# Products with w_in1 in float32 on 64x32 tiles of the array, blocks of 384 tokens, and a second batch that starts like the first

## The chip, the cores and the metric

The kernel runs on one core of a Trainium2 chip. The core has five engines with queues of their own: TensorE (PE; its weight loads are a row of their own, PEld), VectorE (DVE), ScalarE (ACT), GpSimd (POOL) and SyncE (SP), which issues all DMAs here. The metric is the device time of one execution in microseconds (us).

## The reference, cut to what matters

```python
def sm_attn(qq, kk, vv):              # softmax over the keys
    s = scale * np.matmul(qq, kk.transpose(0, 1, 3, 2))
    ...
p_packed = sm_attn(p, k, v)           # 32 packed queries p over 576 keys
out = sm_attn(q, p_packed, p_packed)  # 576 queries q over 32 packed rows
x = out, as (8*576, 512)
h = x @ w_in1;  x = (h * sigmoid(h)) @ w_out1     # 512 -> 2048 -> 512
h = x @ w_in2;  y = (h * cos(h)) @ w_out2         # 512 -> 2048 -> 512
```

There are 8 batches, 8 heads of 64, 576 rows. All four weight matrices arrive as float64, so the kernel reads them as pairs of 32-bit words and makes float32 of them ("conversion").

## The kernel before, in words

**Numbers in two parts.** Large products are made from a high part rounded to float32r and a low part that is what is left: `mm3` (lines 485 to 489) issues low x high, high x low, high x high. `split` (501) makes the parts with a copy on ACT or DVE and a subtraction on DVE or POOL.

**Attention.** Per batch b and half g of the heads, `stage1` (703) makes the 64 packed rows per pair of heads (`ppf`), and `stage2` (769) the probabilities of the 576 queries over them (`a2`). The attention's output is never formed: since x = a2 @ packed, the first MLP's h is a2 @ (packed @ w_in1). So `products` (815) multiplies the packed rows with w_in1, for a quarter s of w_in1's columns at a time (512), and puts the result as two parts into slots of W (`mslot`). For this `stationary` (759) places the packed rows of both batches of a pair in the zero-padded tile L; `parts` (805) moves the two batches' halves out of the bank, 64 partitions at a time: a copy and a subtraction each. Batch 0 alone takes `sole_products` (826).

**Batch 0 and the others.** Batch 0 uses the class `Boot` (629): q and k come on 96 partitions, six rows of 64 on each (1.5 KB runs), and TensorE turns them by products with the identity. All others use `Steady` (585): they come in runs of 32 numbers to the tiles kin, and VectorE turns them (STREAM_TRANSPOSE big<-kin).

**Conversion.** `decode` (517) reads 128x512 float64 numbers into wd (or wde at the start), and makes float32 in wy with one ACT, three or four DVE and one POOL instruction, then `split`s it. Units: 16 of w_in1 (both parts spilled to w1dram, 512 KB, and loaded again for each pair by `w1_load`, 800), 16 of w_out1 (to W), 32 of w_in2 and w_out2 (`w2_unit`, to w2dram).

**First MLP.** A step is one block of tokens and one of 16 column chunks fc: six matmuls into hb (`first`, 853), tanh on ACT, a multiplication on DVE (gf), `split` into g, and three steps later twelve matmuls into the four banks acc. A block is half a batch, 288 tokens, so a pair of batches takes 4 x 16 = 64 steps, and 4 pairs 256. In pair 0 the steps go by quarters of fc, and each quarter's sums are kept apart (ydram, ypart). At a block's end two banks are moved out by ACT and two by DVE into one tile ysb, and one DMA takes it to DRAM.

**Second MLP.** 9 blocks of 512 tokens times 16 steps of 24 matmuls of 512 columns.

**What sets the order.** The program is recorded by `Plan` (79) and put in one static order by a list scheduler with prices (`price`, 151), due times (`due_first`, 964, from DUE, 410), release times, and copies that may go to either of two engines (`either`). Every engine's queue then runs in this order; a waiting instruction holds up all behind it on its engine, SP's DMA issues too. The loop at 1052 to 1074 records, for each pair, the steps of the first MLP, the attention of the next pair's batches (`seconds`), its products (from step 48 of 64 on), and in the last pair the w2 units.

Of the kernel before, what the change touches and what calls it, by code (L numbers as in the profile page):

```python
# [74 lines left out]
class Op:  # L75
    __slots__ = ("choice", "engine", "emit", "cost", "issue", "due", "release", "after", "before")


class Plan:
# [9 lines left out]
    ISSUE, WIRE = 500, 650  # L89

# [60 lines left out]
    def price(self, engine, f, out, ins):  # L151
# [32 lines left out]
    def add(self, engine, f, emit, args, kw):  # L184
# [11 lines left out]
        self.record(engine, run, [self.region(x) for x in outs], [self.region(x) for x in ins], cost, issue)  # L196

# [7 lines left out]
    def record(self, engine, emit, outs, ins, cost, issue):  # L205
# [5 lines left out]
        else:  # L211
# [4 lines left out]
            op.after, op.before, op.choice = [], [], {}  # L216
# [56 lines left out]
    def schedule(self, rank, reverse=False):  # L273
# [40 lines left out]
        while done < n:  # L314
# [5 lines left out]
            for e in queue:  # L320
# [7 lines left out]
                end = free[e] = t + o.cost  # L328
# [50 lines left out]
def attention_mlps_kernel(  # L379
# [17 lines left out]
    P = 128  # L397
    HALF = S // 2
    NB = S // 32
# [10 lines left out]
    DUE = [38e3, 212e3, 392e3, 572e3, 738e3]  # L410
# [33 lines left out]

    ydram = dram.tile([KC, P, NT], F32, name="ydram")
    ypart = [dram.tile([KC, P, 2 * S], F32, name=f"ypart{i}") for i in range(1, NG)]
    w1dram = dram.tile([KC, KC, P, 2, 512], F32, name="w1dram")
# [33 lines left out]
    mask = const.tile([P, 2], F32, name="mask")  # L481
    half_pi = const.tile([P, 1], F32, name="half_pi")
    pbd = const.tile([P, H // 2, 2 * NP], F32, name="pbd")
# [27 lines left out]
    early_wy = tiles(stage, [P, WIDE], I32, "wye", 1)  # L511
# [5 lines left out]
    def decode(src, dst=None, spill=None):  # L517

        wd, y = rings["wd"](), rings["wy"]()
        flat = wd.rearrange("p f t -> p (f t)")  # L520
        parts = flat.rearrange("p (t f) -> p t f", t=2).bitcast(F32R)
        DMA.dma_start(flat.rearrange("p (c f) -> p c f", c=src.shape[1]) if len(src.shape) == 3 else flat, src)
        lo, hi = wd[:, :, 0], wd[:, :, 1]
        yf = y.bitcast(F32)
# [13 lines left out]
    def w1_unit(s, hp, dst):  # L538

        decode(w_in1[hp * P : (hp + 1) * P, 1024 * s : 1024 * (s + 1)], dst, w1dram[s, hp])  # L540

    def wout1_unit(c):
        decode(w_out1[c * P : (c + 1) * P], W[c])

    def w2_unit(c, i):
# [4 lines left out]
        decode(src, None, w2dram[c, i])  # L550
# [11 lines left out]
    Ls = ring(tiles(att, [P, 2, H // 2, 2, 2 * NP], F32R, "L", 1))  # L562
    a2s = ring(tiles(a2p, [P, 2, S], F32R, "a2", 4))

    def place_p(b):
# [8 lines left out]
        for h2 in range(2):  # L574
            r = slice(64 * h2, 64 * h2 + 64)
            V.transpose(pbd[r, :, NP * h2 : NP * h2 + NP], t[r].rearrange("p j d -> p (j d)"))
# [52 lines left out]
    class Boot:  # L629
# [11 lines left out]
        def load(self, n, src):  # L641
            for g in range(2):
                for j in range(2):
# [3 lines left out]
                        src[0, h].rearrange("h (r c) d -> r h (c d)", c=NCH),  # L647
# [37 lines left out]
    def half(b, j):  # L685

        return (b + j) % 2

    ppf = {}
    L = {}  # L690
    a2 = {}

    def scores(keys, queries, rows, bank):

        sts = [bank()[:, :HALF] for _ in range(2)]
        with plan.together():
            for hf, st in enumerate(sts):
                c = slice(hf * HALF, (hf + 1) * HALF)
                for j in range(2):
                    T.matmul(st[rows(j)], keys[:, j], queries[j][:, c], start=True, stop=True)  # L700
        return sts

    def stage1(b, g, bank, mem):
# [5 lines left out]
        sts = scores(pbd[:, 2 * g : 2 * g + 2], kt, lambda j: slice(64 * j, 64 * j + 64), bank)  # L709
# [22 lines left out]
        with plan.together():  # L732
            for c in range(n):
                for j in range(2):
                    for h2 in range(2):
                        h = 32 * (2 * j + h2)
# [12 lines left out]
            mask.unsqueeze(2).to_broadcast([P, 2, D]),  # L749
# [9 lines left out]
    def stationary(b, g):  # L759

        if (b // 2) not in L:
            L[b // 2] = Ls()
        t = ppf[b, g]
        for j in range(2):
            hi, lo = (L[b // 2][:, x, 2 * g + j, half(b, j)] for x in range(2))
            copy(hi, t[:, j])
            combine(lo, t[:, j], f32(hi), ALU.subtract)

    def stage2(b, g, bank, mem):
# [4 lines left out]
        rows = lambda j: slice(64 * half(b, j), 64 * half(b, j) + 64)  # L774
        for hf, st in enumerate(scores(ppf[b, g], qt, rows, bank)):
            V.transpose(sf[:, hf * HALF : (hf + 1) * HALF], st)
# [344 lines left out]
```

## Time and profile before

| | us |
|---|---|
| median of 3 runs | 1641.14 (1639.12 to 1641.47) |
| profiled execution | 1641.7 |
| its span, first to last instruction | 1639.9 |
| TensorE busy | 1578.5 (96%) |
| VectorE busy | 1187.8 (72%) |
| ScalarE busy | 803.8 (49%) |
| GpSimd busy | 343.3 (21%) |

Busy is the time in which an engine has an instruction at work. Matmuls are pipelined, so TensorE can be busy and slower than it could be: the distance between the starts of matmuls tells its pace. Groups of instructions are named output<-inputs by the program's tiles, without buffer numbers. A float32 matmul stands as two instructions in the trace where it runs on a tile of the array.

### The profile page before, as it was taken

The page shows a single profiled execution, that of the slowest core. Times are in us where ns is not written, and L with a number is a line of the kernel's source. Part 1 is how long each engine was busy: PE and PEld are TensorE (multiplying, and loading weights), DVE is VectorE, ACT ScalarE, POOL GpSimd, SP SyncE. Part 2 cuts the span into 40 slices and gives each one's busy share as a digit, 9 for nine tenths or more (in the row PEclk, how much of TensorE's full clock was granted, in tenths as well). Part 3 has the DMA queues.
Part 4 walks back from the last instruction along what each step waited for, and adds up shares of the span by engine and source line. Part 5 has one row for each costly group of instructions (what it writes and reads, how often), then busy time and mean ns, then how long its engine had stood idle before and what let it go on. Part 6 is the DMA issues. An engine that isn't in the chain of part 4 may idle for free.

```text
span 1639.9 us, 25508 instructions
## 1 busy us (share of the span) xinstructions
PE 1578.5 (96%) x9570; PEld 1374.1 (84%) x9570; DVE 1187.8 (72%) x2157; ACT 803.8 (49%) x1584; POOL 343.3 (21%) x311
## 2 busy tenths in 40 slices
PE   8777999999988999999999999999999999999999
PEld 7667988899888999999988888888878888888887
DVE  6999688888688766756356767666676867676665
ACT  5665565645455454644344444444444444444444
POOL 2556232233133411002001101010221111120000
PEclk9889999999999999999999999999999999999999
DMA  8666777854687445524350101000020302010000
GB/s 205 190 236 160 205 203 201 275 168 145 152 221 236 149 115 110 182 83 137 143 195 0 52 1 39 14 26 27 20 71 1 110 20 90 6 47 1 13 14 26
DMA packets 238140, 175.74 MB, mean 107 GB/s; under 512 B 176320, under 2 KB 202688, under 8 KB 238016
## 3 DMA queue, kind: packets, MB, share of 16 engines
q1 hardware_dynamic: 238016, 174.11, 36.1%
q8 instruction: 75, 1.23, 0.3%
q14 instruction: 49, 0.40, 0.1%
HBM read 122.95 MB, written 51.12 MB: 106 GB/s over the span
## 4 chain that ended last, share of the span: by engine, by line
PE 63%; DVE 9%; issue 3%; DMA 2%; ACT 2%; POOL 1%; SPq 0%; DVEq 0%; POOLq 0%; ACTq 0%
PE acc L191 34%; PE hb L191 16%; PE sb L191 7%; PE mb L191 6%; DVE r L191 2%; DVE g L191 1%; ACT r L191 1%; DVE wd L191 1%; DVE big L191 1%; DVE wy L191 1%; DMA kin<-in_q 1%; DVE w L191 1%; DVE gf L191 1%; DVE n L191 1%; DMA yst<-ydram 1%
## 5 line engine op out<-in xcount | busy, mean ns | idle before, releaser
L191 PE MATMUL acc<-g,w 128*128 128x288 f32 x3072 | 472.8, 299 | 12.9 <-DVE ysb L191 5.3
L191 PE MATMUL acc<-w,g 128*128 128x512 f32 x1728 | 473.2, 394 | 2.2 <-DVE o L191 1.4
L191 PEld LDWEIGHTS acc<-g,w 128*128 128x128 f32 x3072 | 432.8, 190 | 27.5 <-DVE ysb L191 6.9
L191 PEld LDWEIGHTS acc<-w,g 128*128 128x128 f32 x1728 | 323.5, 187 | 81.3 <-DVE o L191 3.4
L191 PE MATMUL hb<-a,w 128*128 128x288 f32 x1536 | 264.7, 304 | 29.6 <-DVE w L191 9.7
L191 PEld LDWEIGHTS hb<-a,w 128*128 128x128 f32 x1536 | 227.0, 193 | 45.1 <-DVE gf L191 12.2
L191 ACT ACTIVATE r<-r 128x512 f32<-128x512 f32 x144 | 91.1, 633 | 339.2 <-DVE r L191 339.1
L191 PE MATMUL hb<-y,w 128*128 128x512 f32 x864 | 241.0, 391 | 0.0
L191 POOL TENSOR_TENSOR g<-r,g 128x512 fp32r<-128x512 f32 x49 | 64.9, 1324 | 611.3 <-ACT g L191 611.3
L191 PEld LDWEIGHTS hb<-y,w 128*128 128x128 f32 x864 | 162.1, 188 | 35.2
L191 ACT CAST g<-gf 128x288 fp32r<-128x288 f32 x233 | 100.3, 433 | 157.3 <-PE acc L191 102.0
L191 DVE TENSOR_TENSOR g<-gf,g 128x288 fp32r<-128x288 f32 x173 | 94.6, 548 | 81.3 <-ACT g L191 78.3
L191 DVE SCALAR_TENSOR_TENSOR gf<-gf,hb 128x288 f32<-128x288 f32 x256 | 113.5, 447 | 39.2 <-ACT gf L191 37.7
L191 ACT ACTIVATE gf<-hb 128x288 f32<-128x288 f32 x256 | 104.2, 409 | 69.2 <-PE hb L191 64.7
L191 POOL TENSOR_TENSOR g<-gf,g 128x288 fp32r<-128x288 f32 x83 | 75.7, 912 | 294.9 <-ACT g L191 267.5
L191 DVE SCALAR_TENSOR_TENSOR r<-n,r 128x512 f32<-128x512 f32 x144 | 126.6, 879 | 2.8
L191 PE MATMUL sb<-y,w 128*128 128x512 f32 x432 | 122.5, 391 | 0.0
L191 PE MATMUL mb<-y,w 128*128 128x512 f32 x432 | 121.6, 391 | 0.0
L191 DVE TENSOR_TENSOR r<-r,hb 128x512 f32<-128x512 f32 x72 | 49.5, 687 | 83.3 <-ACT r L191 83.2
L191 ACT ACTIVATE r<-r,half_pi 128x512 f32<-128x512 f32 x144 | 104.3, 724 | 4.2
L191 PEld LDWEIGHTS sb<-y,w 128*128 128x128 f32 x432 | 81.0, 188 | 17.2
L191 PEld LDWEIGHTS mb<-y,w 128*128 128x128 f32 x432 | 81.0, 188 | 17.1
(176 smaller groups left out, 1809.9 us busy)
## 6 DMA issues: line engine op xcount, KB each, us to landing
w<-w1dram SPq DMA_DIRECT2D x52, 512.0 KB, 4.4
w2dram<-wd SPq DMA_DIRECT2D x32, 512.0 KB, 3.4
w<-w2dram SPq DMA_DIRECT2D x32, 512.0 KB, 5.4
wd<-in_moe_w_in SPq DMA_DIRECT2D x24, 512.0 KB, 4.9
wd<-in_moe_w_out SPq DMA_DIRECT2D x20, 512.0 KB, 4.4
ydram<-ysb SPq DMA_DIRECT2D x16, 576.0 KB, 3.5
yst<-ydram SPq DMA_DIRECT2D x36, 256.0 KB, 2.7
out<-o SPq DMA_DIRECT2D x36, 256.0 KB, 2.0
```

The lines of the kernel that those rows point to most:

```text
L191: run = lambda: emit(*[real(x) for x in args], **{k: real(x) for k, x in kw.items()})
```

## The change

Products with w_in1: the packed rows stay float32 (ppf), w_in1 stays float32 (no parts; 256 KB per spill and load), and each batch, head pair and head is a matmul of its own of 64 rows and 32 columns of the array. L, `stationary`, `parts`, `sole_products` are gone; a bank holds 128 partitions of one batch and is moved out whole. `place(b, h2)` swaps the two heads' places for odd batches, in masks, pbd and stage1. Blocks are 384 tokens: three per pair, of which the middle one spans both batches (twelve hb matmuls of 192 columns), so 48 steps a pair, 192 in all; each block's four evictions go to ACT or DVE as the planner likes, into two tiles of a quarter each, with a DMA each. Batch 1 uses Boot and its tiles. The w2 units are released at the planner's 380 us. Its prices and DUE change, and it counts DVE as slowed by a busy POOL.

```diff
@@ prices and schedule
-            passes = 1 if ins[0].dtype == F32R else 4
-            return passes * n / 2.4 * (out.shape[0] / 128) + (14 if out.shape[0] == 128 else 24), 0
+            if ins[0].dtype == F32R:
+                return n / 2.4 + 14, 0
+            return n * out.shape[0] / 128 * (1.67 if out.shape[0] == 128 else 1.2 if ins[0].shape[0] > 64 else 0.6) + 10, 0
...
+                if e == self.DVE and o.sbuf and not reverse and free[self.POOL] > t:
+                    both = min(free[self.POOL] - t, o.cost / self.SHARED)
+                    end += both * (1 - self.SHARED)
...
-    DUE = [38e3, 212e3, 392e3, 572e3, 738e3]
+    DUE = [40e3, 205e3, 378e3, 550e3, 718e3]
@@ conversion
-        d = parts if dst is None else dst
-        split(d, yf)
-        if spill is not None:
-            DMA.dma_start(spill, f32(d))
+        return flat
+
+    def decode_parts(src, dst=None):
+        y = rings["wy"]()
+        flat = decode(src, y)
+        d = flat.rearrange("p (t f) -> p t f", t=2).bitcast(F32R) if dst is None else dst
+        copy(d[:, 0], y.bitcast(F32))
+        V.tensor_tensor(d[:, 1], y.bitcast(F32), f32(d[:, 0]), ALU.subtract)
+        return d
...
+    def w1_unit(s, hp, w):
+        decode(w_in1[hp * P : (hp + 1) * P, 1024 * s : 1024 * (s + 1)], w)
+        DMA.dma_start(w1dram[s, hp], w)
@@ products
-        for hp in range(KC):
-            w = ws[hp] if ws else w1_load(s, hp)
-            bank = (mb, sb)[hp % 2]
-            mm3(bank, heads(L[pr], hp), (w[:, 0], w[:, 1]), True, True)
+    def products(s, bs, ws=None):
+        ws = ws or [w1_load(s, hp) for hp in range(KC)]
+        for kc in range(2):
+            banks = {b: (mb, sb)[(kc + i) % 2] for i, b in enumerate(bs)}
+            with plan.together():
+                for b in bs:
+                    for j in range(2):
+                        for h2 in range(2):
+                            r, c = slice(64 * h2, 64 * h2 + 64), 32 * place(b, h2)
+                            T.matmul(
+                                banks[b][64 * j + c : 64 * j + c + 32],
+                                ppf[b, kc][r, j, c : c + 32],
+                                ws[2 * kc + j][r],
+                                start=True,
+                                stop=True,
+                            )
             for b in bs:
-                r = 64 * half(b, hp % 2)
-                parts(b, hp // 2, s, slice(r, r + 64), bank)
+                m = mslot(b, kc, s)
+                copy(m[:, 0], banks[b])
+                V.tensor_tensor(m[:, 1], banks[b], f32(m[:, 0]), ALU.subtract)
@@ steps of the first MLP
-    ysbs = ring(tiles(gp, [P, KC, HALF], F32, "ysb", 1))
+    ysbs = ring(tiles(gp, [P, TA], F32, "ysb", 2))
...
+        for b in range(2):
+            t0, t1 = max(blk * TA, b * S), min((blk + 1) * TA, (b + 1) * S)
+            if t0 >= t1:
+                continue
+            for kc in range(2):
+                m = mslot(b, kc, fc // 4)
+                a = a2[2 * pr + b, kc]
+                c = slice(t0 - b * S, t1 - b * S)
+                mm3(h[:, t0 - blk * TA : t1 - blk * TA], (m[:, 0, o : o + P], m[:, 1, o : o + P]), (a[:, 0, c], a[:, 1, c]), kc == 0, kc == 1)
...
             for dm in range(KC):
-                if dm % 2:
-                    V.tensor_scalar(t[:, dm], acc[dm][:, :HALF], 0.5, None, op0=ALU.mult)
-                else:
-                    A.activation(t[:, dm], acc[dm][:, :HALF], AF.Copy, scale=0.5)
+                t = ysbs()
+                with plan.either():
+                    A.activation(t, acc[dm][:, :TA], AF.Copy, scale=0.5)
+                    V.tensor_scalar(t, acc[dm][:, :TA], 0.5, None, op0=ALU.mult)
+                DMA.dma_start(dst[dm, :, t0 : t0 + TA], t)
...
-    ysts, yst = lates("yst", F32, 2)
+    ysts, yst = lates("yst", F32, 1)
@@ recording
-    firsts(1, steady, [bank, bank])
-    stationaries(1)
-    products(0, 0, (1,), ws)
-    seconds(1)
+    boot.load("k", k, 1)
+    boot.load("v", v, 1)
+    boot.load("q", q, 1)
+    firsts(1, boot, [bank, bank])
+    products(0, (1,), ws)
+    for g in range(2):
+        stage2(1, g, bank, boot)
...
+            plan.release = LATER
             for c in range(FC):
                 for i in range(2):
                     w2_unit(c, i)
+            plan.release = 0.0
...
-            if o == (31 if pr else 55):
+            if o == (31 if pr else 43):
                 seconds(b0 + 2)
-            if o >= 48 and o % 4 == 3:
-                products(pr + 1, (o - 48) // 4, (b0 + 2, b0 + 3))
+            if o >= 32 and o % 4 == 3:
+                products((o - 32) // 4, (b0 + 2, b0 + 3))
```

On PE, at the products of pair 0 with a later quarter of w_in1 (mb and sb are the two banks, w10 and w11 tiles of w_in1, ppf0 and ppf2 the packed rows of batches 0 and 1), there stands before:

```order
L191 MATMUL acc3_90<-g1_147,w3_98 128x288
L191 MATMUL mb_93<-w10_140,L0_135 128x512 x2
L191 MATMUL sb_94<-w11_141,L0_135 128x512
L191 MATMUL mb_93<-w10_140,L0_135 128x512
L191 MATMUL sb_94<-w11_141,L0_135 128x512 x2
L191 MATMUL hb0_91<-a23_139,w28_102 128x288
```

and now:

```order
L194 MATMUL acc3_90<-g0_150,w3_98 128x384
L194 MATMUL mb_93<-w10_140,ppf0_132 32x512 x2
L194 MATMUL mb_93<-w11_141,ppf0_132 32x512 x2
L194 MATMUL sb_94<-w10_140,ppf2_134 32x512 x2
L194 MATMUL sb_94<-w11_141,ppf2_134 32x512 x2
L194 MATMUL hb0_91<-a22_138,w24_101 128x192
```

Six matmuls on the whole array have become one group of eight on tiles of it, and the hb matmuls after it have 192 columns, since the step belongs to a block that spans two batches.

On SP, in the first loads (bx0, bx1, bx2 are Boot's tiles for k, v and q, kin and vin those of Steady, wd and wde take weights), there stands before:

```order
L191 DMA bx1_151<-in_v 96x2x384 x4
L191 DMA kin0_167<-in_k 32x18x32 x4
L191 DMA kin1_168<-in_k 32x18x32 x4
L191 DMA pin0_118<-in_p 32x4x32
L191 DMA bx2_152<-in_q 96x2x384
L191 DMA pin0_118<-in_p 32x4x32 x3
L191 DMA bx2_152<-in_q 96x2x384 x2
L191 DMA vin0_169<-in_v 128x4x64 x4
L191 DMA bx2_152<-in_q 96x2x384
L191 DMA vin0_169<-in_v 64x2x64 x2
L191 DMA kin0_167<-in_k 32x18x32 x4
L191 DMA kin1_168<-in_k 32x18x32 x4
```

and now:

```order
L194 DMA bx1_156<-in_v 96x2x384 x2
L194 DMA bx2_157<-in_q 96x2x384
L194 DMA bx0_155<-in_k 96x2x384 x2
L194 DMA pin0_119<-in_p 32x4x32 x4
L194 DMA bx2_157<-in_q 96x2x384 x2
L194 DMA bx1_156<-in_v 96x2x384 x2
L194 DMA bx0_155<-in_k 96x2x384 x2
L194 DMA bx1_156<-in_v 96x2x384 x2
L194 DMA wde2_115<-in_moe_w_out 128x1024
L194 DMA wde3_116<-in_moe_w_out 128x1024
```

Batch 1's k and v now go into the tiles that batch 0 has used, ahead of the first loads of w_out1, and its q behind two of them.

On ACT, at the end of a block (ysb takes the banks acc, gf the tanh of hb), there stands before:

```order
L191 CAST w19_2095<-sb_94 64x512
L191 ACTIVATE ysb0_149<-acc0_87 128x288
L191 ACTIVATE ysb0_149<-acc2_89 128x288
L191 CAST w27_2097<-mb_93 64x512
L191 CAST g0_146<-gf0_144 128x288
L191 ACTIVATE gf1_145<-hb1_92 128x288
```

and now:

```order
L194 ACTIVATE ysb0_153<-acc0_87 128x384
L194 ACTIVATE ysb1_154<-acc1_88 128x384
L194 ACTIVATE wd1_110<-wd1_110 128x512
L194 ACTIVATE gf0_148<-hb0_91 128x384
L194 CAST g2_152<-gf0_148 128x384
L194 ACTIVATE gf1_149<-hb1_92 128x384
L194 CAST g0_150<-gf1_149 128x384
L194 ACTIVATE gf0_148<-hb0_91 128x384
L194 ACTIVATE ysb0_153<-acc2_89 128x384
L194 ACTIVATE ysb1_154<-acc3_90 128x384
L194 ACTIVATE gf1_149<-hb1_92 128x384
```

All four banks of a block are now moved out by ACT (82 of 84 in the whole program), two and two, and the second two wait for the DMAs of the first two.

## Rows read from the trace of the kernel before

**Rows 1.** VectorE's busy share in 40 slices of the span, on the page.

```profile
DVE  6999688888688766756356767666676867676665
```

**Rows 2.** Stretches: start:end, length; PE, PEld, DVE, ACT, POOL busy (xcount); clock; DMA.

```profile
60.00:160.00 100.00, 76.52 (x481) 68.42 (x480) 98.73 (x164) 63.58 (x132) 61.45 (x46) 0.94 0.65 199
160.00:440.00 280.00, 270.48 (x2138) 250.23 (x2138) 226.64 (x464) 157.13 (x365) 81.54 (x82) 0.99 0.69 198
440.00:640.00 200.00, 188.90 (x1489) 174.83 (x1488) 148.03 (x297) 104.09 (x241) 56.36 (x57) 0.98 0.61 169
640.00:840.00 200.00, 200.00 (x1449) 194.59 (x1450) 119.19 (x236) 91.69 (x202) 16.84 (x16) 1.00 0.47 150
840.00:1640.00 800.00, 793.85 (x3447) 645.13 (x3445) 552.29 (x906) 354.85 (x575) 105.68 (x85) 1.00 0.10 32
```

**Rows 3.** Timeline of TensorE, two steps late in the first MLP: start, us, instructions.

```profile
758.36 1.76 PE L191 MATMUL acc<-g,w 128*128 128x288 f32 x12
...
760.76 1.50 PE L191 MATMUL acc<-g,w 128*128 128x288 f32 x10
```

**Rows 4.** Stretches of TensorE, instructions on hb alone.

```profile
60.00:160.00 100.00, 29.07 (x153) 0.94 0.65 199
160.00:440.00 280.00, 95.08 (x551) 0.99 0.69 198
440.00:640.00 200.00, 64.94 (x381) 0.98 0.61 169
```

**Rows 5.** Stretches of TensorE, products with L alone.

```profile
160.00:440.00 280.00, 19.73 (x66) 0.99 0.69 198
440.00:640.00 200.00, 14.41 (x48) 0.98 0.61 169
```

**Rows 6.** Stretches of TensorE, attention on big alone.

```profile
160.00:440.00 280.00, 28.95 (x418) 0.99 0.69 198
440.00:640.00 200.00, 20.99 (x302) 0.98 0.61 169
```

**Rows 7.** Timeline of TensorE at a product with w_in1.

```profile
206.16 0.86 PE L191 MATMUL sb<-w,L 128*128 128x512 f32 x3
206.85 0.43 PE L191 MATMUL acc<-g,w 128*128 128x288 f32 x2
```

**Rows 8.** Timeline of TensorE at the scores of one batch's half.

```profile
195.30 0.91 PE L191 MATMUL acc<-g,w 128*128 128x288 f32 x5
196.14 0.71 PE L191 MATMUL sb<-big,pbd 128*64 128x288 f32 x4
...
197.26 0.67 PE L191 MATMUL acc<-g,w 128*128 128x288 f32 x3
```

**Rows 9.** VectorE groups: line, operation, tiles, shapes, xcount; busy us, mean ns; idle before.

```profile
L191 DVE SCALAR_TENSOR_TENSOR gf<-gf,hb 128x288 f32<-128x288 f32 x256 | 113.5, 447 | 39.2 <-ACT gf L191 37.7
L191 DVE TENSOR_TENSOR g<-gf,g 128x288 fp32r<-128x288 f32 x173 | 94.6, 548 | 81.3 <-ACT g L191 78.3 <-POOL L L191 1.5
...
L191 DVE STREAM_TRANSPOSE big<-kin 128x576 f32<-128x576 f32 x56 | 42.9, 765 | 8.5 <-DMA kin<-in_q 6.3 <-PE mb L191 2.1
L191 DVE TENSOR_TENSOR w<-sb,w 64x512 fp32r<-64x512 f32 x62 | 42.6, 686 | 5.6 <-ACT w L191 4.3
...
L191 DVE TENSOR_SCALAR ysb<-acc 128x288 f32<-128x288 f32 x56 | 23.2, 445 | 2.1 <-PE acc L191 2.1
```

**Rows 10.** Timeline of TensorE in the start, warm-up matmuls.

```profile
17.20 1.23 PE L191 MATMUL mb<-ident 128*128 128x64 f32 x10
18.27 0.82 PE L191 MATMUL acc<-ident,ba 128*96 128x128 f32 x6
```

**Rows 11.** The chain of waits at 399 us: start, us, what.

```profile
399.15 3.53 DMA wd<-in_moe_w_in
```

**Rows 12.** TensorE's group of the second product, columns as in rows 9.

```profile
L191 PE MATMUL acc<-g,w 128*128 128x288 f32 x3072 | 472.8, 299 | 12.9 <-DVE ysb L191 5.3 <-ACT ysb L191 3.4 <-DVE w L191 2.4
```

**Rows 13.** DMA issues on the page: xcount, KB each, median us to landing.

```profile
ydram<-ysb SPq DMA_DIRECT2D x16, 576.0 KB, 3.5
```

More of the change, by code (lines that the diff above doesn't have):

```diff
@@ L75 @@
 class Op:
[L76 removed]
+    __slots__ = ("choice", "engine", "emit", "cost", "issue", "due", "release", "after", "before", "sbuf")
 class Plan:
@@ L196, in add @@
         self.record(engine, run, [self.region(x) for x in outs], [self.region(x) for x in ins], cost, issue)
+        self.ops[-1].sbuf = all(str(raw(x).space).endswith("SBUF") for x in outs + ins)
     @contextmanager
@@ L215, in record @@
                 op.cost += self.TURN
-            op.after, op.before, op.choice = [], [], {}
+            op.after, op.before, op.choice, op.sbuf = [], [], {}, False
             op.release = self.release
@@ L683, in values, with scores @@
             return lambda c, h2, j: self.x["v"][:CH, 4 * g + 2 * j + h2, c, :]
-    def half(b, j):
-        return (b + j) % 2
     ppf = {}
-    L = {}
     a2 = {}
-    def scores(keys, queries, rows, bank):
+    def scores(keys, queries, bank):
         sts = [bank()[:, :HALF] for _ in range(2)]
@@ L757, in stage1 @@
         ppf[b, g] = t
[L759 to L767, printed above, removed]
     def stage2(b, g, bank, mem):
@@ L773, in stage2 @@
         sf = s.rearrange("p n r -> p (n r)")
-        rows = lambda j: slice(64 * half(b, j), 64 * half(b, j) + 64)
-        for hf, st in enumerate(scores(ppf[b, g], qt, rows, bank)):
+        for hf, st in enumerate(scores(ppf[b, g], qt, bank)):
             V.transpose(sf[:, hf * HALF : (hf + 1) * HALF], st)
@@ L838, in attention_mlps_kernel @@
     steps = []
     for pr in range(NPAIR):
-        runs = [(b, 0, FC, 0) for b in (0, 1)]
+        runs = [(blk, 0, FC, 0) for blk in range(NA)]
         if pr == 0:
-            runs = [(b, s * FC // NG, (s + 1) * FC // NG, s) for s in range(NG) for b in (0, 1)]
-        for b, c0, c1, part in runs:
-            for hf in range(2):
-                steps += [(2 * pr + b, hf, c, c == c0, c == c1 - 1, part) for c in range(c0, c1)]
+            runs = [(blk, s * FC // NG, (s + 1) * FC // NG, s) for s in range(NG) for blk in range(NA)]
@@ L846, in attention_mlps_kernel @@
+        for blk, c0, c1, part in runs:
+            steps += [(pr, blk, c, c == c0, c == c1 - 1, part) for c in range(c0, c1)]
     NS = len(steps)
-    PER = 4 * FC
+    PER = NA * FC
     LAG = 3
-    gfs = ring(tiles(gp, [P, HALF], F32, "gf", 2))
-    gs = ring(tiles(gp, [P, 2, HALF], F32R, "g", LAG))
-    ysbs = ring(tiles(gp, [P, KC, HALF], F32, "ysb", 1))
+    gfs = ring(tiles(gp, [P, TA], F32, "gf", 2))
+    gs = ring(tiles(gp, [P, 2, TA], F32R, "g", LAG))
+    ysbs = ring(tiles(gp, [P, TA], F32, "ysb", 2))
@@ L1005, in firsts @@
             stage1(b, g, banks[g], mem)
-    def stationaries(b):
-        for g in range(2):
-            stationary(b, g)
     def seconds(b):
```

130 lines of the change are left out of this document (51 added, 79 removed).

## The prediction

> **What bounds the kernel now.** I read the busy table by stretches first, then the pace of the matmuls at the end of the first MLP, then counts of single tiles, then the chain of waits. Four stretches come out. From 60 to 160 us VectorE is busy 98.73 of 100 us and TensorE waits for it [rows 1, 2]. From 160 to 640 us TensorE is busy 94 to 97% and VectorE 74 to 81% [rows 2]. From 640 us on TensorE has no gap [rows 2]. The last 800 us are the second MLP, whose matmuls the change leaves alone.
>
> Busy TensorE isn't TensorE at its pace, so I count work. Where nothing holds it, the first MLP starts a step every 2.40 us (758.36 to 760.76), 18 matmuls of 288 columns, 133 ns each [rows 3]. A step has six matmuls into hb. From 160 to 440 us there are 551 of these, 91.8 steps, 220 us at that pace; 66 products with w_in1 at 0.23 us (three from 206.16 to 206.85) are 15 us, and 29 us are attention on the tiles named big [rows 4 to 7]. That is 264 of 280 us. From 440 to 640 us it is 381/6 x 2.40 = 152, 48 x 0.23 = 11, and 21, so 184 of 200 us. So 32 us are lost there. From 60 to 160 us it is 153/6 x 2.40 = 61 of 100 us; less a few for products and attention, some 30 us are lost. All that faster helper engines can give back is these 62 us, and TensorE's own work can change besides.
>
> **The products with w_in1.** Before: 204 matmuls of 512 columns, 204 x 0.23 = 47 us of TensorE [rows 7]. After: 256 float32 matmuls of 32x512, in 30 groups of eight (two batches) and four groups of four. No row shows float32 on 64x32 tiles. The nearest shows 128x64 tiles: four score matmuls of 288 columns, written by two tiles at a time, go from 196.14 to 197.26 us, 1.12 us [rows 8]. Without some 0.1 us of change of tiling that is two waves of 0.5 us, or 0.9 us for a wave of 512 columns. Entering costs 0.17 us (the five matmuls from 195.30 are worth 0.67, and the first score starts 0.84 after them [rows 8]); I add 0.3 us a group for entering and leaving. The eight tiles of a group share no 64x32 place of the array. In one wave a group costs 1.2 us, and 34 x 1.2 = 41 us: a gain of 6. Four at a time it is 2.1 us, 30 x 2.1 + 4 x 1.2 = 68 us: a loss of 21. Two at a time, 3.9 us, is a loss of 78, and one at a time, 7.5 us, one of 194. I take one wave, since in the nearest rows all the tiles that the mode has in use run at once.
>
> The Trainium skill's page TensorEngine Tiling (Array Packing), section Restrictions and Gotchas, speaks against this: different row tiles can't access one PSUM bank at the same time, and here both row halves of a batch write one bank. By that rule the four matmuls of a batch would follow one another; no row of this trace has two row halves at work, so it neither agrees nor disagrees. It is the first rival below.
>
> **What the products take off the other engines.** The results were moved out in halves of 64 partitions: 126 subtractions on VectorE at 0.686 us (the 62 of the row of sb, the mb ones alike) become 64 of the same width on 128 partitions, and an instruction's time follows its columns: minus 42 us of VectorE [rows 9]. The copies beside them halve likewise on ScalarE. The stationary parts L go, and w_in1 needs no low part. Eight of 56 VectorE transposes of 0.765 us go with the second batch (minus 6) [rows 9], for sixteen evictions that the planner put on ScalarE. Of the block evictions 54 of 56 leave VectorE (minus 23 of 23.2 us) [rows 9].
>
> **Blocks of 384.** 256 steps become 192. The matmuls carry the same columns: 133 ns for 288 is 120 ns at 2.4 GHz and 13 of overhead, so one of 384 is 173 ns and a full step 3.12 us. But a third of the steps has a block that spans both batches, with twelve hb matmuls of 192 columns. By columns these are 93 ns. The warm-up matmuls bound it from the other side: ten of 64 columns go from 17.20 to 18.27 us, 107 ns each, four times their columns [rows 10], so something under 111 ns per 128 stationary columns does not go faster there. I take 111: 128 x 3.12 + 64 x (12 x 0.173 + 12 x 0.111) = 399 + 218 = 617 us against 256 x 2.40 = 614, plus 3 (minus 10 by 93 ns). The Trainium skill's page TensorE: Matmul & The Clock Gate, section LDWEIGHTS (loading the stationary operand), gives columns / 1.2 ns for a load, by which 128 columns are 107 ns; the 107 ns of the warm-up agree. On VectorE 256 x 0.447 becomes 192 x 0.55, and 173 subtractions of 0.548 become 142 of 0.64 [rows 9]: minus 12 us with their copies.
>
> Counted over the order with these means, VectorE's work up to the last step falls from 690 to 611 us. What matters is where. Up to the middle of pair 0 (32 of 64 steps, 24 of 48) it falls from 164 to 151 us: minus 9 for batch 1's attention, minus 7 evictions of products, minus 6 block evictions, minus 2 for L, plus 10 since four more weight tiles are converted by then, and small ones. VectorE is the bound there, so **minus 13 us**. Bounds: 0, if batch 1 becomes a latency chain (second rival); minus 20, if the lighter GpSimd lets it run faster.
>
> From there to the end of pair 0 VectorE falls from 94 to 73 us. From pair 1 to its end it falls from 176 to 110, as w2 units leave: there they are in the chain of waits, as at 399.15 us, 3.53 us of a w2 load [rows 11]. But from the middle of pair 2 on the same units come back, and VectorE has 165 us of work in pair 2 against 159. And in the first half of pair 3, where before it had 57 us of work, it has 77, as many as 24 steps last at TensorE's pace. So of the 32 lost us of 160 to 640 I count 18 as given back, mostly in the first part, and 5 as lost again in pair 3: **minus 13** (bounds minus 28 and plus 8).
>
> **Waits.** Before, a block's four evictions shared one tile, and TensorE's second product waited 5.3 us for VectorE's share of them and 3.4 for ScalarE's [rows 12]. Now there are two tiles of a quarter: the third eviction waits until the first has landed in DRAM, 3.5 us for four times the size [rows 13], and it stands on ScalarE with a tanh behind it (the order on ACT). The order on PE works ahead on acc0 and acc1 and lets acc2 and acc3 follow, which covers some 2 us. 21 block ends against 28: 0, bounds minus 5 and plus 20 (1 us an end). Batch 1's transposes add TensorE work before 100 us, where it waits anyway. In the second MLP only one y tile instead of two; a block lasts 16 steps in some 88 us (800 us over nine blocks [rows 2]) and refills four chunks: 0.
>
> Sum: -6 +3 -13 -13 = -29 us. The profiled execution took 1641.7 us (span 1639.9); the median of the runs shown is 1641.1, 0.6 less. So **1612 us**.
>
> **The rivals.** *The tiles don't run side by side.* Without the products the sum is -23. Four at a time gives 1641 - 23 + 21 = 1639 us; two at a time 1641 - 23 + 78 = 1696 and one at a time 1641 - 23 + 194 = 1812, both slower. The sign turns once a group takes over (47 + 23) / 32 = 2.2 us (34 groups, the four small ones counted half). For it: no row has two row halves together, and the bank is shared. Against it: the column tiles in the nearest rows do run together. I give four at a time 0.14 and fewer than that 0.04.
>
> *The gain is given back.* Batch 1 uses the tiles of batch 0, so its first stage starts only when batch 0's second has left them; the first block needs only batch 0, the second block, four steps later, needs both, where before eight steps came first. Between those two the order holds 35 us of VectorE work, but if the chain is longer than that, the start gains nothing; and if the w2 units, now 31 of 32 behind the middle of the first MLP, make VectorE the bound in pairs 2 and 3, another 10 to 15 us go. Then it is 1641 - 29 + 13 + 10 = 1635, or up to 1645. For it: VectorE full at 60 to 160 us; against it: decoding fills such gaps. Chance 0.2.
>
> *The change is too small in effect to see*, since TensorE takes as much as before: it holds if neither of the 13 us comes, which is the same case at its slower end.
>
> **The numbers.** Forecast 1612, chance 0.62, its own range 1592 to 1626. Four at a time 0.14 (1639, about half of it faster by more than 3 us), given back 0.2 (1635, about 0.6 of it faster), fewer at a time 0.04. About 0.2%, 3 us, is what this measurement can tell from no change. Faster: 0.62 + 0.07 + 0.12 = 0.81; within: 0.06; slower: 0.13. The 80% range is 1584 to 1641: below, the start and the stretch to 640 us at their better bounds; above, the two middle cases.
>
> **What would show it.** Right: eight 32x512 matmuls of a group start within a few ns and the group is over in 1.3 us; the middle of pair 0 comes 13 us earlier; the first MLP ends at about 811 us instead of 840 and the second still takes 800 us; TensorE's idle from 160 to 440 us is halved. Wrong: groups of 2 us or more, VectorE idle before 100 us on batch 1's tiles, VectorE full after 500 us, or ScalarE waiting for ysb to land at every block end. Steps of the spanning blocks of 3.2 us instead of 3.4 would show that loads of 128 columns don't bind.

## The result, and the profile after

The changed kernel takes 1603.2 us (median of four runs, 1601.3 to 1604.5) against 1641.3 for the kernel before: ratio 0.9767, 95% interval 0.975 to 0.9784, so 38 us faster, where 1612 was forecast. Its profiled execution has a span of 1602.1 us at a mean granted clock of 0.989 (before 1639.9, 0.987).

The stretches of the changed kernel, with the columns of [rows 2], and VectorE's slices from its page, which answer [rows 1]:

```profile
DVE  5998667553689678884456767676776777676766
```

```profile
60.00:160.00 100.00, 80.70 (x533) 68.93 (x532) 89.47 (x143) 60.10 (x117) 47.12 (x33) 0.86 0.60 178
160.00:440.00 280.00, 280.00 (x2110) 252.63 (x2109) 160.88 (x314) 122.67 (x264) 15.88 (x14) 1.00 0.39 94
440.00:640.00 200.00, 198.23 (x1433) 176.55 (x1432) 155.59 (x293) 106.28 (x214) 59.68 (x48) 0.99 0.63 182
640.00:818.00 178.00, 175.01 (x1117) 164.82 (x1117) 112.31 (x196) 78.88 (x153) 31.44 (x26) 1.00 0.59 199
818.00:1602.00 784.00, 780.50 (x3442) 644.96 (x3440) 547.69 (x914) 353.71 (x571) 95.00 (x78) 1.00 0.10 33
```

From 160 us on TensorE has next to no idle time by its busy column (1.8 us up to 640, 3.0 from there to 818, 3.5 behind), and VectorE fell by 66 us between 160 and 440. The first MLP's last twelve products with w_out start at 817.4 us (840.4 before): 23 us of the 38. The other 15 are where nothing was expected: from there to the end of the span, the second MLP takes 784.7 us instead of 799.5.

Starts of the tanh into gf, on ScalarE, at fractions of the first MLP's steps, in us; the quarters are the four pairs:

| | first | 1/16 | 1/8 | 1/4 | 1/2 | 3/4 | last | last product |
|---|---|---|---|---|---|---|---|---|
| before | 59 | 120 | 176 | 281 | 479 | 670 | 831 | 840.4 |
| changed | 53 | 130 | 174 | 276 | 455 | 646 | 806 | 817.4 |

At an eighth the changed kernel is 2 us ahead, after pair 0 it is 5, after pair 1 24, and from there these marks show nothing won or lost. By them the first MLP's gain is almost all pair 1's: 179 us instead of 198. They mark steps of ScalarE, though, and TensorE's work can slip over them: further down its matmuls are counted.

A group of products, on TensorE's timeline (answers [rows 7]): 

```profile
489.57 0.86 PE L194 MATMUL hb<-a,w 128*128 128x384 f32 x4
490.36 0.63 PE L194 MATMUL sb<-w,ppf 64*32 64x512 f32 x4
490.38 0.63 PE L194 MATMUL mb<-w,ppf 64*32 64x512 f32 x4
490.81 0.61 PE L194 MATMUL sb<-w,ppf 64*32 64x512 f32 x4
490.84 0.61 PE L194 MATMUL mb<-w,ppf 64*32 64x512 f32 x4
491.38 0.44 PE L194 MATMUL hb<-a,w 128*128 128x384 f32 x1
```

Each float32 matmul stands there as two records. All eight tiles, the two row halves of one bank among them, start within some 50 ns (6 to 7 ns from one to the next); the second records follow 0.45 us later, and 1.02 us after the first start the next matmul runs. That is one wave, and all 30 groups of eight in the trace start like this. The Trainium skill's page TensorEngine Tiling (Array Packing), section Restrictions and Gotchas, says that different row tiles can't access one PSUM bank at the same time; this trace doesn't agree for tiles that write different partitions of the bank, as these do: by that rule the four tiles of a bank would need at least two turns. An estimate from the 0.45 us of a record: 0.9 us more a group.

Two steps of a block that spans both batches, late in the first MLP (answers [rows 3]):

```profile
741.86 2.28 PE L194 MATMUL acc<-g,w 128*128 128x384 f32 x12
743.98 1.48 PE L194 MATMUL hb<-a,w 128*128 128x192 f32 x12
745.29 2.28 PE L194 MATMUL acc<-g,w 128*128 128x384 f32 x12
```

A step is 745.29 - 741.86 = 3.43 us, the 3.4 of the prediction: twelve matmuls of 192 columns take 1.31 us, 109 ns each, and not the 93 that the prediction worked out from their columns. This is close to the 111 that it took for loads of 128 stationary columns.

The groups of VectorE and TensorE that answer [rows 9, 12]:

```profile
L194 PE MATMUL acc<-g,w 128*128 128x384 f32 x2304 | 461.5, 342 | 4.3 <-ACT ysb L194 2.4 <-POOL g L194 0.9 <-DVE g L194 0.5
L194 DVE SCALAR_TENSOR_TENSOR gf<-gf,hb 128x384 f32<-128x384 f32 x192 | 105.0, 548 | 63.6 <-ACT gf L194 62.1
L194 DVE TENSOR_TENSOR g<-gf,g 128x384 fp32r<-128x384 f32 x142 | 85.5, 602 | 99.6 <-ACT g L194 98.0
L194 DVE STREAM_TRANSPOSE big<-kin 128x576 f32<-128x576 f32 x48 | 36.7, 765 | 4.7 <-PE mb L194 2.3 <-DMA kin<-in_k 2.1
L194 DVE TENSOR_TENSOR w<-sb,w 128x512 fp32r<-128x512 f32 x32 | 21.7, 680 | 3.4 <-ACT w L194 3.3
```

The durations are as taken (548 and 602 ns for 0.55 and 0.64 us, 680 for a full-height subtraction), and the waits of these products for ysb went from 8.7 us (5.3 and 3.4 in [rows 12]) to 2.4.

### The profile page after: what moved, and what is told of

It is laid out like the page before. It is cut to its first block, busy times and chain, and to the rows that moved or that the text cites. A ratio compares the mean times of both kernels' runs of the same rounds, so it can differ in the third digit from the quotient of the medians.

```text
span 1602.1 us, 24478 instructions
## 1 busy us (share of the span) xinstructions
PE 1565.0 (98%) x9320; PEld 1348.7 (84%) x9320; DVE 1108.7 (69%) x1957; ACT 755.6 (47%) x1388; POOL 267.4 (17%) x216
## 4 chain that ended last, share of the span: by engine, by line
PE 88%; DVE 8%; issue 1%; ACT 1%; DMA 1%; POOL 1%; SPq 0%; DVEq 0%; POOLq 0%; ACTq 0%
PE acc L194 47%; PE hb L194 24%; PE sb L194 9%; PE mb L194 9%; DVE w L194 1%; DVE wy L194 1%; DVE wde L194 1%; DVE wd L194 1%; DVE g L194 1%; DVE big L194 1%; DVE r L194 1%; DVE gf L194 0%; DVE rsb L194 0%; ACT r L194 0%; SPq L194 0%
## 5 line engine op out<-in xcount | busy, mean ns | idle before, releaser
L194 PE MATMUL acc<-g,w 128*128 128x384 f32 x2304 | 461.5, 342 | 4.3 <-ACT ysb L194 2.4
L194 PE MATMUL acc<-w,g 128*128 128x512 f32 x1728 | 464.4, 389 | 0.1
L194 PEld LDWEIGHTS acc<-g,w 128*128 128x128 f32 x2304 | 400.1, 190 | 36.9 <-issue 20.9
L194 PE MATMUL hb<-a,w 128*128 128x384 f32 (+1 forms) x1536 | 271.2, 311 | 21.7 <-ACT a L194 11.1
L194 PEld LDWEIGHTS hb<-a,w 128*128 128x128 f32 x1536 | 237.0, 194 | 35.5 <-ACT a L194 13.6
L194 ACT CAST g<-gf 128x384 fp32r<-128x384 f32 x171 | 87.7, 513 | 176.9 <-PE acc L194 150.7
L194 DVE TENSOR_TENSOR g<-gf,g 128x384 fp32r<-128x384 f32 x142 | 85.5, 602 | 99.6 <-ACT g L194 98.0
L194 DVE SCALAR_TENSOR_TENSOR gf<-gf,hb 128x384 f32<-128x384 f32 x192 | 105.0, 548 | 63.6 <-ACT gf L194 62.1
L194 ACT ACTIVATE gf<-hb 128x384 f32<-128x384 f32 x192 | 94.0, 490 | 91.9 <-PE hb L194 90.8
L194 POOL TENSOR_TENSOR g<-gf,g 128x384 fp32r<-128x384 f32 x50 | 59.7, 1194 | 352.0 <-ACT g L194 288.7
```

Source lines behind the costliest of these rows:

```text
L194: run = lambda: emit(*[real(x) for x in args], **{k: real(x) for k, x in kw.items()})
```

## The experiments

### Why is the second MLP faster?

TensorE's work there is the same in both kernels. What differs is where the tiles lie in SBUF: the constants grew by 1056 bytes per partition and the tiles of the first MLP by 1536, so the built programs put W (w2 in the second MLP) and y 1056 bytes lower and g2 1536 bytes higher. An acc matmul has g2 stationary and w_out moving, an h matmul w_in stationary and y moving. Unused tiles shift one or the other. The line is added behind the first MLP's tiles (gp: moves a2 and g2) or behind the constants (const: moves W and y).

```diff
 b_left:               + gp.tile([P, 128], F32, name="pad")
 b_right32, a_right32: + const.tile([P, 8], F32, name="pad")
 b_left32, a_left32:   + gp.tile([P, 8], F32, name="pad")
```

Expected of b_left:

> The kernel before with one unused tile of 512 bytes per partition behind the tiles of the first MLP, which moves a2, n, r and g2 up by 512 bytes; the weights in W stay where they are and PE's order stays as it is. In the profile of the changed kernel the second MLP takes 784 us instead of 799, because a matmul into acc starts 227 ns before the next instead of 234; g2 lies there at 128 of 1024 bytes, before at 640, and here at 128. Theory A (where g2, the stationary operand, lies decides): acc matmuls 227 ns, second MLP 784 us, 1626 us in all. Theory B (where w_out, the moving operand, lies decides: 32 bytes off a multiple of 64 before, on it after): 234 ns, 799 us, 1641. Theory C (no address; the changed kernel's second MLP is faster for another reason, as its single y tile): 234 ns, 1641.

Of b_right32 and of a_right32:

> The kernel before with one unused tile of 32 bytes per partition among the constants, which moves every tile of W and y down by 32 bytes, to a multiple of 64 bytes as in the changed kernel; g2 stays where it is. Theory B (w_out off a multiple of 64 bytes costs 7 ns a matmul): acc matmuls 227 ns instead of 234, second MLP 784 us, 1626 in all, or a little less if the first MLP's products with w_out gain too. Theory A (g2's address): 234 ns, 799 us, 1641. Theory C (no address): 1641.

> The changed kernel with the same unused tile of 32 bytes among the constants, which moves W and y off the multiple of 64 bytes again. Theory B: acc matmuls 234 ns instead of 227, second MLP 799 us instead of 784, 1618 us in all. Theories A and C: 227 ns, 784 us, 1603 in all.

Of b_left32 and a_left32, after the three above:

> The kernel before with one unused tile of 32 bytes per partition behind the tiles of the first MLP: a2 and g2 now lie 32 bytes off a multiple of 64, as W and y do. Runs so far: W moved by 32 bytes onto the multiple takes the acc matmuls of the second MLP from 234 to 227 ns (and back in the changed kernel, 227 to 231), moving g2 by 512 bytes does nothing, and the h matmuls, where both operands lie off the multiple, take 227. Theory D (it costs 7 ns when the stationary and the moving operand lie differently against 64 bytes): acc matmuls 227 ns here, second MLP some 10 us shorter, about 1630 in all, though the first MLP's acc matmuls have g on and W off as before. Theory B (only w_out as the moving operand off the multiple costs it): 234 ns as before, 1641.

> The changed kernel with the same tile of 32 bytes: a2 and g2 lie 32 bytes off the multiple of 64, W, y and g on it. Theory D: acc matmuls of the second MLP 231 to 234 ns instead of 227, 10 to 13 us longer, about 1615 in all. Theory B: 227 ns, 1603.

Measured (ratio to the kernel before in the same runs; a step is 24 matmuls, from one run of four acc matmuls behind the h run to the next such):

| kernel | W, y modulo 64 bytes | g2 | step us | time us | ratio, interval |
|---|---|---|---|---|---|
| before | 32 | 0 | 5.52 | 1641 | 1 |
| b_left | 32 | 0 | 5.52 | 1642.0 | 0.9998 (0.998 to 1.0017) |
| b_right32 | 0 | 0 | 5.44 | 1633.2 | 0.9945 (0.9928 to 0.9963) |
| b_left32 | 32 | 32 | 5.44 | 1634.0 | 0.9956 (0.9939 to 0.9972) |
| changed | 0 | 0 | 5.44 | 1603.2 | 0.9767 (0.975 to 0.9784) |
| a_right32 | 32 | 0 | 5.54 | 1619.9 | 0.9862 (0.9833 to 0.989) |
| a_left32 | 0 | 32 | 5.54 | 1616.1 | 0.9849 (0.9832 to 0.9866) |

TensorE's timeline of the kernel before, of b_right32, b_left32, the changed kernel and a_left32, each from such a start to the next; only these two rows of the step are shown:

```profile
1041.01 1.09 PE L191 MATMUL acc<-w,g 128*128 128x512 f32 x4
...
1046.53 1.09 PE L191 MATMUL acc<-w,g 128*128 128x512 f32 x4
```

```profile
1041.94 1.07 PE L191 MATMUL acc<-w,g 128*128 128x512 f32 x4
...
1047.38 1.07 PE L191 MATMUL acc<-w,g 128*128 128x512 f32 x4
```

```profile
1042.23 1.07 PE L191 MATMUL acc<-w,g 128*128 128x512 f32 x4
...
1047.67 1.07 PE L191 MATMUL acc<-w,g 128*128 128x512 f32 x4
```

```profile
1042.07 1.07 PE L194 MATMUL acc<-w,g 128*128 128x512 f32 x4
...
1047.51 1.07 PE L194 MATMUL acc<-w,g 128*128 128x512 f32 x4
```

```profile
1044.33 1.09 PE L194 MATMUL acc<-w,g 128*128 128x512 f32 x4
...
1049.87 1.09 PE L194 MATMUL acc<-w,g 128*128 128x512 f32 x4
```

Theory A falls with b_left (a large shift of g2 does nothing). B, that w_out's place alone decides, holds for both right32 runs and falls with the left32 pair: moving g2 by 32 bytes cures the kernel before and spoils the changed one. C, that no address matters, falls with them too, since the pads change nothing else: in the built programs the instructions of all computing engines are the same, in the same order. D holds in all seven: the acc matmuls start every 227 ns where the two operands lie alike, and some 230 to 235 where they lie 32 bytes apart. 144 steps by 0.08 to 0.10 us are 12 to 14 us, and the spans of a_right32 and a_left32 (1614.9 and 1614.3) are 12 to 13 above the 1602.1: most of the second MLP's 15.

In the kernel before, the cure is worth only 6 to 8 us of the medians; by the traces the second MLP is 8 us shorter in b_right32 and in b_left32. Some of the rest is lost at block ends: TensorE's waits from 860 to 1600 us, before and in b_right32 (total, times, longest):

```profile
PE acc L191 <- DVE o L191: 1.4, 2, 1.2
PE acc L191 <- ACT o L191: 0.6, 1, 0.6
```

```profile
PE acc L191 <- DVE o L191: 3.0, 5, 1.3
PE acc L191 <- ACT o L191: 1.4, 2, 1.0
```

The waits grow by 2.4 us; what else takes from the 12 isn't shown. The changed kernel shows no wait in that stretch.

### Why did the start gain so little?

Windows from 80 to 140 and 140 to 180 us, of the kernel before and of the changed one (columns as in [rows 2]):

```profile
80.00:140.00 60.00, 45.67 (x286) 42.02 (x284) 59.23 (x96) 37.48 (x76) 36.21 (x28) 0.91 0.61 196
140.00:180.00 40.00, 34.11 (x219) 30.77 (x220) 35.84 (x62) 22.76 (x51) 22.41 (x19) 0.96 0.75 214
```

```profile
80.00:140.00 60.00, 41.82 (x222) 36.64 (x223) 55.93 (x86) 33.65 (x67) 28.87 (x20) 0.80 0.56 168
140.00:180.00 40.00, 40.00 (x258) 37.98 (x257) 27.70 (x49) 21.57 (x45) 11.12 (x9) 0.96 0.45 134
```

VectorE's work did fall, by 11 us over these two (and by 15 from the start to the eighth, 155.4 to 140.7 us busy, while its idle time grew from 21 to 34). But from 80 to 140 us TensorE is busy for less time than before, and from 140 on it is full and VectorE no longer the bound. TensorE's waits from 60 to 180 us in the changed kernel:

```profile
PE hb L194 <- ACT a L194: 7.8, 2, 4.7
PE hb L194 <- DVE gf L194: 4.0, 2, 3.2
PE acc L194 <- ACT ysb L194: 2.4, 1, 2.4
PE hb L194 <- DVE a L194: 2.1, 2, 1.2
```

The tiles a are batch 1's. TensorE's first matmuls that need the second of them, in the changed kernel and before:

```profile
94.03 0.74 PE L194 MATMUL hb<-a,w 128*128 128x192 f32 x2 [4.68 <-ACT a L194]
```

```profile
92.59 0.53 PE L191 MATMUL hb<-a,w 128*128 128x288 f32 x2 [4.07 <-ACT a L191]
```

So batch 1 is ready no earlier than before. But until then there are only four steps of 384 tokens that do without it, 4 x 3.12 = 12.5 us of TensorE, where there were eight of 288, 8 x 2.40 = 19.2. The order on VectorE has 13 units of weight conversion between the fourth gf and the fifth, the first that needs batch 1, and VectorE is full until 97 us. The gaps cost clock as well. These are the stretches between 53 and 174 us in which TensorE was granted 0.50 (1.2 of 2.4 GHz): the longest one, in which it waits for batch 1 half of the time, and the sum of the four in the changed kernel, then the sum of the three between 59 and 176 us before (TensorE alone):

```profile
85.50:102.60 17.10, 8.49 (x34) 0.50 0.82 255
sum 30.70, PE 21.02; mean PE 5.25
```

```profile
sum 13.60, PE 11.96; mean PE 3.99
```

TensorE worked 21.0 us at half the clock instead of 12.0. Its 192-column matmuls start every 213 ns there instead of 109, so by an estimate half of such time is lost, and some 4 to 5 us of the start went there. The run a_steady gives batch 1 its tiles of before:

```diff
-    boot.load("k", k, 1)
-    boot.load("v", v, 1)
-    boot.load("q", q, 1)
-    firsts(1, boot, [bank, bank])
+    firsts(1, steady, [bank, bank])
...
-    for g in range(2):
-        stage2(1, g, bank, boot)
+    seconds(1)
```

> The changed kernel, but batch 1's attention goes as it did before (tiles of its own, turned by VectorE instead of TensorE), so that it need not wait until batch 0 has left its tiles; eight VectorE transposes of 0.77 us come back. My prediction gave the start 13 us; the traces show 2 (at an eighth of the first MLP 176 us before, 174 after), with TensorE idle at 80 to 140 us waiting for batch 1's a2 tiles. Theory S1 (the chain of batch 1 behind batch 0 on shared tiles holds the start back): the eighth of the first MLP comes 5 to 10 us earlier, about 1595 in all. Theory S2 (the order holds batch 1's work back on a VectorE that is full of conversion, whichever tiles it uses): no gain, or 6 us lost for the transposes, 1603 to 1610.

Measured: 1602.8 us, ratio 0.9765 (0.9732 to 0.9797): the same time as the changed kernel. The sixteenth comes at 119 us instead of 130 and the eighth at 170 instead of 174, but the first gf only at 64 instead of 53, and at the end of the first MLP 3 us are left. S1 is right about the place (the chain holds the early steps back, by up to 11 us) and wrong about the total, where S2 came nearer: of what a_steady was earlier at the sixteenth, most is gone again at the eighth. The run doesn't tell the shared tiles from the order of VectorE, since both changed with it.

### What the later w2 conversion does

```diff
 a_rel0:  -    LATER = 380e3
          +    LATER = 0e3
 b_rel300 (before, around the loop of w2 units):
          +            plan.release = 300e3
          +            plan.release = 0.0
 as_rel460, as_rel540 (on a_steady): LATER = 460e3, 540e3
```

> The kernel before with one part of the change alone: no w2 unit starts before 300 us of the planner's time, which puts the first one at the middle of the first MLP (34 units of 64 ahead of it, as in the changed kernel). Quarters of the first MLP from first to last gf (the four pairs): before 222, 198, 191, 160 us; changed 222, 179, 191, 160. Theory R1 (the w2 units that leave pair 1 are its gain of 19 us, and before has room for them in pairs 2 and 3 no more than the changed kernel has): pair 1 some 182 us, pair 2 and 3 together 10 to 20 us longer, 1635 to 1645 in all: the later conversion alone gives nothing, and the lighter VectorE work of the rest of the change pays for it. Theory R2 (the later conversion is a gain by itself): pair 1 shorter, pairs 2 and 3 as before, 1620 to 1628.

> The changed kernel without that part: w2 units may start as soon as there is room, so 26 of 32 stand ahead of the middle of the first MLP, as before. Theory R1: pair 1 back to 190 to 198 us, pair 2 10 to 15 us shorter (176 to 181), 1600 to 1610 in all, as the changed kernel. Theory R2: pair 1 longer and pairs 2 and 3 as they are, 1613 to 1622.

Measured: b_rel300 1632.8 us, 0.9951 (0.9933 to 0.997), a_rel0 1607.5 us, 0.98 (0.9773 to 0.9827). Pairs in us: before 222, 198, 191, 161 and b_rel300 222, 190, 191, 164; changed 223, 179, 191, 160 and a_rel0 228, 190, 179, 160. In the changed kernel R1's numbers hold: 11 to 12 us move from pair 1 to pair 2 or back. The total changes by 4 us (medians; 8 by the spans), and these lie ahead of pair 1: in a_rel0 the first gf is 2 us later and pair 0 takes 5 more, with five w2 units in it where the changed kernel has none. In the kernel before pair 1 gains 8 of its 19 by the release alone, pair 2 pays nothing and pair 3 pays 3, so neither theory's number holds there; the total gains 7 us (medians; 3.5 by the spans of the two profiled executions). The other 11 of pair 1 come with the rest of the change.

> The changed kernel with batch 1's attention on tiles of its own (as in the run with that alone: 1602.75 us) and the w2 units later still, from 460 us of the planner's time, so that 22 of 32 fall into pair 3, which has no attention of a next pair. In that run pair 2 takes 193 us and pair 1 179 for the same TensorE work, so the units in pair 2 would cost some 12 us. Theory W1 (VectorE has room for them in pair 3): pair 2 183 to 187 us, pair 3 at most 163, 1594 to 1600 in all. Theory W2 (what leaves pair 2 comes back in pair 3 or at the start of the second MLP, which needs the last units): 1602 to 1610.

> The same with the w2 units from 540 us of the planner's time: none before the last quarter, and 13 of 32 behind the three quarters' middle are left for the second MLP's first block. Theory W1: pair 2 181 us; pair 3 as long as before only if the units left over fit beside the second MLP: 1592 to 1600. Theory W2: the second MLP's first block waits for weights, 1605 to 1625.

Measured: 1615.3 us, 0.9843 (0.9816 to 0.987), and 1690.6 us, 1.0301 (1.0272 to 1.033). W1 falls twice. Pair 2 takes 190 us in both, even in as_rel540, which stores two w2 units in its second half and none in its first, so the units are not what makes it longer than pair 1. And the units left over stop the second MLP's first block: TensorE's waits from 640 to 920 us are 9.4 us for sb in as_rel460, whose first MLP is not longer. TensorE's waits from 780 to 920 us in as_rel540:

```profile
PE sb L194 <- ACT y L194: 63.3, 2, 62.2
PE sb L194 <- DVE r L194: 6.3, 1, 6.3
```

Most of what makes pair 2 longer can be read from the trace of the changed kernel: TensorE has more to do in it. Its groups of acc and of products from 276.3 to 455.0 us (pair 1) and from 455.0 to 645.9 (pair 2):

```profile
L194 PE MATMUL acc<-g,w 128*128 128x384 f32 x575 | 114.5, 340 | 0.0
L194 PE MATMUL mb<-w,ppf 64*32 64x512 f32 x48 | 6.4, 601 | 0.0
```

```profile
L194 PE MATMUL acc<-g,w 128*128 128x384 f32 x597 | 119.5, 342 | 0.0
L194 PE MATMUL mb<-w,ppf 64*32 64x512 f32 x68 | 9.1, 602 | 0.0
```

These are 20 or so acc matmuls of 0.173 us and 2.5 groups of products of 1.02 us more (each group has eight records on mb and eight on sb), and seven hb matmuls: some 7 of the 12 us, by an estimate from these prices. They are matmuls that the order lets slip over the marks into pair 2. The same holds for a_rel0, whose pair 2 has some 40 acc matmuls less than the changed kernel's. So the pairs' times tell a move of work from a gain only in part.

### Blocks of 384, and the products

```diff
 a_288:   -    TA = 384
          +    TA = 288
          -            if o == (31 if pr else 43):
          +            if o == (41 if pr else 57):
          -            if o >= 32 and o % 4 == 3:
          -                products((o - 32) // 4, (b0 + 2, b0 + 3))
          +            if o >= 48 and o % 4 == 3:
          +                products((o - 48) // 4, (b0 + 2, b0 + 3))
 a_twice: -                for b in bs:
          +                for b in bs * 2:
```

(a_288 also has 2400 for 3120 in the due times.)

> The changed kernel with blocks of 288 tokens instead of 384 (256 steps, no block over two batches; the places of the second half of a batch's attention and of the products within a pair are scaled to 64 steps). By the working of my prediction the blocks of 384 cost TensorE 3 us and save VectorE and ScalarE 12 us each over the first MLP. Theory F1 (after the change TensorE binds the first MLP, so the 384 cost what their 192-column matmuls cost): 1597 to 1603. Theory F2 (the fewer, wider instructions on VectorE are what gave the middle stretch back): 1606 to 1618, with TensorE idle again at 160 to 640 us.

> The changed kernel with every group of products with w_in1 run twice into the same banks (the second writes the same values): 34 groups more, 256 float32 matmuls of 32x512. In the trace a group takes 1.1 us of TensorE. Theory T1 (TensorE binds from 140 us on, so a group costs what it lasts): 30 groups behind 140 us by about 0.95 us (two more half waves of 0.43 us, no more entering), 25 to 35 us longer, 1630 to 1638. Theory T2 (the products lie in waits for other engines): under 10 us longer, below 1613.

Measured: a_288 1611.5 us, 0.9816 (0.9797 to 0.9835), 7 us over the changed kernel by the spans (8 by the medians) and all of it in the first MLP. F2's number holds, and the place is pair 2: 202 us instead of 191. Its stretches, where TensorE and VectorE are to be compared with the rows above:

```profile
160.00:440.00 280.00, 277.42 (x2394) 250.80 (x2393) 167.03 (x359) 130.27 (x320) 27.04 (x27) 1.00 0.40 95
440.00:640.00 200.00, 190.03 (x1545) 171.75 (x1543) 156.24 (x299) 98.14 (x224) 60.32 (x52) 0.97 0.59 166
```

TensorE is idle for 10 us from 440 to 640, with VectorE as busy as with 384. In pair 2 it waits for ScalarE's big (3.7 us) and a (2.2) and VectorE's gf (3.3), beside the w2 units. That the wider blocks win because VectorE has fewer instructions beside these units is argued from this and not shown alone: with other blocks the whole order is planned anew.

a_twice took 1626.8 us, 0.9907 (0.9891 to 0.9924): 24 us over the changed kernel by the medians, 21 by the spans, and 20 at the end of the first MLP. A doubled group lasts 1.88 us on TensorE's timeline, 0.86 more than a single one, so 30 groups behind 140 us are 26 us, and four fifths of that reach the end. Nearer to T1 than to T2, under T1's range: most of what a group lasts is on the path.

No kernel of these beats the changed one by more than the measurement tells.

## Why the prediction was right, and where it was wrong

The forecast of 1612 us, 29 less than the profiled execution, missed the changed kernel by 9 us. The first MLP gained 23 us where all 29 were forecast, and the second 15 where none was. Term by term:

- **Products, -6: right, and too small.** One wave, 1.02 us a group where 1.2 was taken, so the groups take 34 x 1.02 = 35 us instead of 47: minus 12. The rival of tiles that don't run side by side is out. a_twice shows that this time counts.
- **Blocks of 384, +3: the term right, the rest of the account wrong.** The 192-column matmuls go at 109 ns and a spanning step takes 3.43 us, as forecast. The row that the price was taken from didn't show it, though: in the same trace the warm-up matmuls of 128 columns start every 213 ns, twice the 107 of those with 64, so their columns alone explain the 107. And VectorE's 12 us from the wider blocks were held to be inside the other terms, while a_288 shows that the blocks as a whole are worth 7 us, in pair 2.
- **The start, -13: failed.** At an eighth 2 us were gained. The step that failed is "VectorE is the bound there, so minus 13 us": VectorE's work fell as counted, by 15 us, but its idle time grew by 12, and TensorE had to wait for batch 1 until as late as before, with fewer steps to fill the time and longer at the lower clock. That is the second rival's chain. a_steady shows its place, and it could have been read from the order, with 13 units ahead of the first step that needs batch 1.
- **160 to 640 us, -13: about right in its sum.** From the eighth to the end of the first MLP 21 us were gained, where this term, the products and the blocks make 16; the products' 6 us more account for the rest. By the gf marks they are pair 1's, but some of that is work that slipped into pair 2. The 5 us lost again in pair 3 came at least in part: TensorE, which had no gap from 640 to 818 us before, has 3.0 us of them, all behind VectorE. The second rival's other half, w2 units that take another 10 to 15 us in pairs 2 and 3, is out: TensorE waits 1.8 us in pair 2. That the w2 units' leaving is a gain is shown only in part: 4 to 8 us of the total in the changed kernel, 3.5 to 7 in the one before.
- **Waits, 0: right.** Nothing was lost: TensorE waited 2.4 us for ysb instead of 8.7, a little better than the term's better bound.
- **Second MLP, 0: failed.** 15 us were gained, some 13 of them because the change happened to move W onto the place modulo 64 bytes that g2 has. The term looked at gaps alone, and the pace of the matmuls, which is what changed, stands in no busy column. Without that, a_left32 and a_right32 take 1616 and 1620 us, by their spans 25 to 26 us less than before: the sum of the named terms, -29, was 3 to 4 us off. That it came so near is partly luck, since a start 11 us too large and a remainder of the first MLP 5 us too small offset each other in part.

The lower end of the 80% range, 1584, isn't the sum that it names either: 1612 less 7 for the start and 15 for the stretch to 640 us is 1590.

The three causes that experiments isolate are the operands' place (12 to 13 us by spans), the blocks of 384 (7) and the later w2 (4 to 8). Each was measured by taking it out of the changed kernel alone, so they need not add up. If they do, 10 to 14 us are left for the products and the lighter VectorE work, which were not run alone. An estimate for the products: of their 12 us less, four fifths reach the end as in a_twice, some 10 us.

## What to carry to other kernels

A stage that an edit leaves alone can still change its pace, because buffers that grow elsewhere move its tiles: compare the start-to-start time of its matmuls before and after, and try a 32-byte pad before looking for a cause in the schedule. Work taken off the engine that is full shortened the start by 2 of 15 us here, since the next steps needed a chain that ended no earlier: before counting freed time as gained, look in the order for what the next step of the bound engine waits for, and how much work is left to do until it comes.

## What the hardware showed that was not expected

Float32r matmuls of 512 columns with 128 stationary columns start every 227 ns or some 230 to 235, by how the two operands lie to each other in SBUF: those into acc are fast 256 bytes apart modulo 512 and slow 224 or 288 apart, and the h matmuls, always 0 apart, are fast. Other distances were not tried, so whether 64 bytes is the unit is open. In the first MLP of the kernel before, where W as the stationary operand and g as the moving one lie 32 bytes apart as well, the matmuls of 288 columns take 133 ns, and 132 with b_right32's pad: there it costs 1 ns at most. In the changed kernel a_right32's pad takes those of 384 columns from 173 to 175. Why it depends on which operand is stationary, or on the columns, is open too.

Eight float32 tiles of 64x32, with both row halves of a batch writing one bank, ran in one wave in all 30 groups: the eighth starts 46 to 51 ns behind the first.
